# Second MLP's weight sums ordered behind the first MLP's gates, stores ordered behind loads, x loaded in pieces

## The chip, the cores and the metric

The kernel runs on one core of one Trainium2 chip. The metric is the device time of one execution in microseconds; before the change it is 837.95 us, the median of three runs (836.85 to 838.01).

## The reference, cut to what matters

A linear attention feeds two MLPs. q, k and v are float32; the four weight matrices are float64 and reach the chip as their bits:

```
q_s = softmax(q, over head_dim); k_s = softmax(k, over seq)      # 4 batches x 8 heads x 576 x 64
x   = q_s @ (k_s^T v), heads side by side                        # 2304 tokens x 512
h   = x @ w_in;   g = h - tanh(h);            x = g @ w_out      # first MLP, 512 -> 2048 -> 512
h   = x @ w_in2;  g = max(h,0)+log1p(exp(-|h|)); out = g @ w_out2   # second MLP
```

## The kernel before

Every product is made from three float32r matmuls: an operand is split into a high part (a cast on ScalarE) and a low part (a subtraction on VectorE), and high by low, low by high and high by high are summed in PSUM.

**Prologue and first MLP.** The 2304 tokens are cut into five blocks of 512, 256, 512, 512 and 512 (blocks 0 to 4). For each block the loop over 16 slices f of the hidden dimension makes one *step*: `hidden` (L460, 12 matmuls), `gate` (L469 to L472: tanh on ScalarE, g on VectorE, gh on ScalarE, gl on VectorE) and `mid_out` (L487 to L489, 12 matmuls into four PSUM accumulators x). Hidden and gate run two steps ahead of mid_out. Steps are numbered 0 to 79 through all blocks. At a block's last step the four accumulators are evicted to SBUF tiles `x2s` (two buffers; chunks 0 and 2 on VectorE, L496, chunks 1 and 3 on ScalarE, L494), and each is stored to DRAM (`x2d`). The next block's first mid_out waits for these evictions, chunk by chunk. Between the steps, `kv_task` and `x_task` prepare the attention output of the next block.

**Weights of the second MLP.** They are prepared while the first MLP runs, in 16 *pairs* of slices: eight of `w2_in_task` (tiles `rawi`, `sums`) and eight of `w2_out_task` (`rawo`, `sumo`). A pair loads two raw tiles of 0.5 MB, converts float64 bits to float32 (L138 on ScalarE, L143 and L144 on VectorE), makes four sums (they belong to a Strassen-Winograd form of the second MLP's products: seven products instead of eight), splits seven pieces (tiles `stage`, L225 and L226) and stores these to DRAM (`formsi`, `formso`). A task is a generator; the loop calls each running task once per step (`advance`). The table at L702 to L704 starts a pair every three steps from step 28 on. But a scheduler places the instructions of each engine by its own modelled times, and nothing holds a pair's instructions back to the step at which they were written.

**Second MLP.** Three groups s of 768 tokens. `x2_task` loads x from DRAM (tile `xs`, L529) and splits it into seven operands `xf`. Then come units A (hidden products, L557) and units B (output products, L658 to L660): 8 x 7 of each per group. Each unit uses one weight piece `wf` of 256 KB that `load_form` (L549) loads eight units ahead, into a ring of eight buffers. `last_parts` (L639, L640) splits the gates for units B, five units ahead. `last_out` evicts results to tiles `ot` and issues their stores (L677) at once. Group s+1's x is loaded during the units B of group s.

All DMAs are issued by SyncE's queue (SPq), in its order: an issue that waits holds back everything behind it. Engine queues, too, run in the order that the scheduler wrote.

Of the kernel before, what the change touches and what calls it, by code (L numbers as in the profile page):

```python
# [16 lines left out]
ALU = mybir.AluOpType  # L17
# [4 lines left out]
def linear_attention_two_mlps(  # L22
# [28 lines left out]
    nc = tc.nc  # L51
    B, H, S, D = q.shape
    NT, DM = out.shape
# [7 lines left out]
    NC = DM // P  # L61
# [28 lines left out]
    def f32(ap):  # L90
        return ap.bitcast(F32)
# [5 lines left out]
    NFORM = 7  # L97
# [114 lines left out]
    PN = NF // 2  # L212
# [43 lines left out]

    OUT_FORM = (2, 0, 3, 4, 5, 1, 6)

    def w2_out_task(p):

        raws = [raw_tile(f"rawo1_{f}").rearrange("p c f -> p (c f)") for f in PAIRS[p]]
        for raw, f in zip(raws, PAIRS[p]):
            load_out(raw, w2_out, f)
        yield
        yield
        w0, w1 = (convert(raw).rearrange("p (s f) -> p s f", s=2) for raw in raws)
        yield
        sums = f32(raw_tile(f"sumo{p}").rearrange("p c f -> p (c f)")).rearrange("p (s f) -> p s f", s=4)
        t2, t3, t1, t4 = (sums[:, i] for i in range(4))
        b11, b12, b21, b22 = w0[:, 0], w0[:, 1], w1[:, 0], w1[:, 1]  # L270
        nc.vector.tensor_tensor(t1, b12, b11, op=ALU.subtract)
        nc.vector.tensor_tensor(t2, b22, t1, op=ALU.subtract)
        nc.vector.tensor_tensor(t3, b22, b12, op=ALU.subtract)
        nc.vector.tensor_tensor(t4, b21, t2, op=ALU.subtract)
        yield
        split_to(forms[1], p, ((0, w1), (2, w0[:, :1])))
        yield
        split_to(forms[1], p, ((3, sums[:, :2]), (5, sums[:, 2:])))
        yield
# [167 lines left out]

    ghl = {}
    acc = {}
    tanh = [None]  # L450

    def hidden(i, f, step):
        n = SIZES[i]
# [10 lines left out]
    def gate(i, f, h):  # L464
        n = SIZES[i]
        g = main.tile([P, NMAX], F32, tag="g", name=f"g{i}_{f}", bufs=2)[:, :n]
        gh = main.tile([P, NMAX], F32R, tag="gh", name=f"gh{i}_{f}", bufs=3)[:, :n]
        gl = main.tile([P, NMAX], F32R, tag="gl", name=f"gl{i}_{f}", bufs=3)[:, :n]
        tanh[0] = nc.scalar.activation(g, h, AF.Tanh)  # L469
        nc.vector.tensor_tensor(g, h, g, op=ALU.subtract)  # L470
        nc.scalar.copy(gh, g)  # L471
        nc.vector.tensor_tensor(gl, g, f32(gh), op=ALU.subtract)  # L472
        ghl[i, f] = gh, gl

    x2d = [dram.tile([P, NC, n], F32, tag=f"x2d{i}", name=f"x2d{i}") for i, n in enumerate(SIZES)]
# [29 lines left out]
    columns = [[] for _ in range(NS)]  # L505
    chunks = []
    for i in range(NB):
        for j in range(JS[i]):
            s, at_ = divmod(len(chunks), W // P)
# [14 lines left out]
    def x2_task(s):  # L524


        xs = late["xs"].tile([P, NC, W], F32, tag="xs", name=f"xs{s}", bufs=1)
        for i, of, n, to in columns[s]:
            nc.sync.dma_start(out=xs[:, :, to : to + n], in_=x2d[i][:, :, of : of + n])  # L529
        yield  # L530
        b11, b12, b21, b22 = (xs[:, k : k + 2, t : t + HW] for k in (0, 2) for t in (0, HW))
        t1, t2 = (late["xs"].tile([P, 2, HW], F32, tag=f"t{n}", name=f"t{n}_{s}", bufs=1) for n in (1, 2))
        nc.vector.tensor_tensor(t1, b12, b11, op=ALU.subtract)
        nc.gpsimd.tensor_tensor(b12, b22, b12, op=ALU.subtract)
        yield
        nc.vector.tensor_tensor(t2, b22, t1, op=ALU.subtract)
        yield
        for k, of in enumerate((b11, b21, t2, b12, t1, b22)):
            split(s, k, of, nc.vector)
            yield  # L540
            if k == 1:
                nc.gpsimd.tensor_tensor(b21, b21, t2, op=ALU.subtract)
        split(s, 6, b21, nc.vector)

    def load_form(unit):
        kind, n, k = unit[:3]
        t = late["wf"].tile([P, 2, 2 * P], F32R, tag="wf", name="wf_" + "_".join(map(str, unit)), bufs=8)
        of = forms[0][n % PN][:, k] if kind == "A" else forms[1][unit[3]][:, OUT_FORM[k]]
        nc.sync.dma_start(out=f32(t), in_=of)  # L549
        wf[unit] = t  # L550

    def product(a, n, k, first):
        w, x = wf.pop(("A", n, k)).rearrange("p h (c f) -> p h c f", c=2), xf[n // PN, k]
# [87 lines left out]

    NT2 = HW // P
    last = {}

    def last_out(s, k, p):

        if p == 0 and k in (0, 1):
            last["m" if k else "one"] = [
                ps.tile([P, 512], F32, tag=tag, name=f"{'m' if k else 'one'}{s}_{j}", bufs=4 if tag == "acc" else 2)
                for j, tag in enumerate(("acc", "a", "a") if k else ("acc", "acc", "acc"))  # L650
            ]
        g, w = gs.pop((s, k, p)), wf.pop(("B", s, k, p))
        for j in range(NT2):
            one, m = (last[name][j][:, : DM // 2] if name in last else None for name in ("one", "m"))
            a = m if k in (1, 3, 6) else one
            c = slice(j * P, (j + 1) * P)
            first = p == 0 and k in (0, 1, 3)
            nc.tensor.matmul(a, g[:, 1, c], w[:, 0], start=first, stop=False, skip_group_check=True)  # L658
            nc.tensor.matmul(a, g[:, 0, c], w[:, 1], start=False, stop=False, skip_group_check=True)  # L659
            nc.tensor.matmul(a, g[:, 0, c], w[:, 0], start=False, stop=p == PN - 1, skip_group_check=True)  # L660
            if p == PN - 1:
                with tc.high_priority():
                    if k in (0, 2, 4):
                        u = last["u", k, j] = late["g"].tile([P, DM // 2], F32, tag=f"v{k}_{j}", name=f"v{s}_{k}_{j}")
                        nc.scalar.activation(u, one, AF.Copy, scale=1.0 / WS)
                    if k == 5:
                        t = late["g"].tile([P, DM // 2], F32, tag="o", name=f"ot{s}_{k}_{j}", bufs=6)
                        nc.scalar.activation(t, one, AF.Copy, scale=1.0 / WS)
                    elif k in (1, 4, 6):
                        u = last["u", {1: 0, 4: 4, 6: 2}[k], j]  # L670
                        t = late["g"].tile([P, DM // 2], F32, tag="o", name=f"ot{s}_{k}_{j}", bufs=6)
                        nc.vector.scalar_tensor_tensor(t, m, 1.0 / WS, u, op0=ALU.mult, op1=ALU.add)
                if k in (1, 4, 5, 6):
                    half, cols = k in (4, 6), k in (4, 5)
                    i, b = chunks[s * (W // P) + half * NT2 + j]
                    rows = out[BASE[i] + b : BASE[i] + SIZES[i] : JS[i], :]
                    nc.sync.dma_start(out=rows[:, cols * DM // 2 : (cols + 1) * DM // 2], in_=t)  # L677


    running = []  # L680
# [12 lines left out]
    def at(block, step, make):  # L693
        starts.setdefault(block * NF + step, []).append(make)
# [5 lines left out]
        if f >= PRE and f % 2 == 0:  # L700
            at(0, f - 8, lambda f=f: w_task(f // 2))
    for p in range(PN):  # L702
        at(2, 3 * p - 4, lambda p=p: w2_in_task(p))
        at(2, 3 * (PN + p) - 4, lambda p=p: w2_out_task(p))  # L704
    for i in range(NB - 1):
        for hp in range(NHP):
            if i < B - 1:
# [69 lines left out]
    for s in range(NS):  # L777
# [6 lines left out]
        n = (s + 1) * PN  # L784
# [10 lines left out]
    x2 = None  # L795
    loads = iter([u for u in UNITS if u[0] != "M"])
    for n in range(min(starts), NB * NF - 2):
# [14 lines left out]
        while n >= -2 and len(gated) < min(n + 3, len(steps)):  # L812
            i, f = steps[len(gated)]
            gate(i, f, hidden(i, f, len(gated)))
            gated.append((i, f))
        if n >= 0:
            i, f = steps[n]
# [35 lines left out]
    with tc.issue_after(tables.ins):  # L853
        x2 = None
        for unit in UNITS:
            if unit[0] == "M":
                next(first_mlp)
                continue
            if unit == ("A", 0, 5):
                assert next(first_mlp, None) is None  # L860
                main_stack.close()
                stacks["g"] = pool("g")
            if unit[0] == "A":
                _, n, form = unit
                if form == 0:
                    pairs[n] = hidden_pair(n)
                next(pairs[n])
            else:
                _, s, form, p = unit
                if (form, p) == (0, 0):  # L870
                    for ahead in backs[done : done + AHEAD]:
                        last_parts(*ahead[1:])
                    x2 = x2_task(s + 1) if s < NS - 1 else None
                    if x2:
                        next(x2)
                at_ = form * PN + p
                ahead = backs[done + AHEAD] if done + AHEAD < len(backs) else None
                if ahead and ahead[1] == s:
                    last_parts(*ahead[1:])
                done += 1  # L880
                last_out(s, form, p)
                if x2 and at_ in (20, 23, *range(26, 47, 3)):
                    next(x2, None)
            for u in itertools.islice(loads, 1):
                load_form(u)
    for key in ("g", "h", "wf", "xf", "xs"):
        stacks[key].close()

# [31 lines left out]
```

## Time and profile before

| what | us |
|---|---|
| median of three runs | 837.95 |
| profiled execution, its time | 840.5 |
| its span | 838.7 |
| PE (TensorE matmul) busy | 816.2 (97%) |
| DVE (VectorE) busy | 596.7 (71%) |
| ACT (ScalarE) busy | 445.6 (53%) |
| mean granted TensorE clock | 0.996 of full speed |

TensorE is the engine that is nearly always busy, so the profile is read for the places where it waits or runs at its lower clock, and for what stands in the queues of the engines that it waits for. The span leaves out 1.8 us of the execution's own time. Blocks 0 to 4 end at about 133, 192, 292, 391 and 481 us of the span; units A and B follow to the end.

### The profile page before, as it was taken

What the parts mean: (1) busy time and instruction counts of PE and PEld (TensorE: products, weight loads), DVE (VectorE), ACT (ScalarE), POOL (GpSimd) and SP (SyncE); (2) the same over time, 40 slices, a digit from 0 to 9 for tenths busy, and PEclk for the clock granted to TensorE, in tenths of its full rate; (3) what the DMA queues carried; (4) which work ended last, traced back from release to release, by engine and by line L of the source; (5) the groups of instructions that cost most, each with busy time, mean ns of one, the idle gap of its engine ahead of it and who ended that gap; (6) DMA issues with size and microseconds to landing.
All of it is one profiled execution on the core that took longest, in us unless ns stands there. A gap on an engine that the chain in (4) does not pass through costs nothing.

```text
span 838.7 us, 14211 instructions
## 1 busy us (share of the span) xinstructions
PE 816.2 (97%) x5068; PEld 737.1 (88%) x5068; DVE 596.7 (71%) x1134; ACT 445.6 (53%) x791; POOL 28.7 (3%) x46
## 2 busy tenths in 40 slices
PE   7999999999999979999999999999999999999998
PEld 6778888898878768888888899999999999999998
DVE  6899987898789864444253277996278995477963
ACT  4888765765666653232242355755255654355553
POOL 5000000000000000001011000100000000000000
PEclk9999999999999989999999999999999999999999
DMA  9978668778667770003022388787988788888886
GB/s 244 353 222 249 191 213 288 233 236 275 243 237 253 267 267 19 13 14 124 1 76 101 110 260 254 241 264 269 313 254 257 229 272 265 285 253 254 245 262 188
DMA packets 118311, 180.22 MB, mean 215 GB/s; under 512 B 28128, under 2 KB 59360, under 8 KB 118240
## 3 DMA queue, kind: packets, MB, share of 16 engines
q1 hardware_dynamic: 118240, 179.30, 66.8%
q8 instruction: 41, 0.67, 0.3%
q14 instruction: 30, 0.25, 0.1%
HBM read 140.47 MB, written 38.80 MB: 214 GB/s over the span
## 4 chain that ended last, share of the span: by engine, by line
PE 73%; DVE 10%; DMA 8%; ACT 5%; issue 2%; SPq 1%; DVEq 0%; ACTq 0%
PE h L460 16%; PE one L557 10%; PE two L557 8%; PE x L487 5%; PE x L488 5%; PE x L489 5%; PE one L658 3%; PE one L660 3%; PE one L659 3%; DMA rawo<-in_moe_w_out_dram 3%; PE m L658 3%; PE m L660 3%; PE m L659 3%; ACT rawo L138 2%; DVE stage L226 1%
## 5 line engine op out<-in xcount | busy, mean ns | idle before, releaser
L460 PE MATMUL h<-xh,i 128*128 128x512 f32 (+1 forms) x640 | 199.5, 377 | 1.4 <-DVE g L470 1.3
L460 PEld LDWEIGHTS h<-xh,i 128*128 128x128 f32 x640 | 117.9, 190 | 22.9 <-DVE g L470 1.7
L487 PE MATMUL x<-gh,o 128*128 128x512 f32 (+1 forms) x320 | 118.7, 371 | 5.9 <-DVE x2s L496 5.9
L460 PE MATMUL h<-xl,i 128*128 128x512 f32 (+1 forms) x320 | 119.0, 372 | 0.0
L488 PE MATMUL x<-gl,o 128*128 128x512 f32 (+1 forms) x320 | 118.5, 370 | 0.0
L489 PE MATMUL x<-gh,o 128*128 128x512 f32 (+1 forms) x320 | 118.3, 370 | 0.0
L557 PE MATMUL one<-xf,wf_A 128*128 128x384 f32 x576 | 109.0, 335 | 0.2 <-DMA wf_A<-formsi 0.2
L639 ACT CAST gs<-g 128x384 fp32r<-128x384 f32 x144 | 72.6, 512 | 64.9 <-PE one L660 30.1
L557 PEld LDWEIGHTS one<-xf,wf_A 128*128 128x128 f32 x576 | 100.3, 188 | 0.7 <-issue 0.5
L640 DVE TENSOR_TENSOR gs<-g,gs 128x384 fp32r<-128x384 f32 x144 | 79.6, 561 | 27.2 <-ACT gs L639 27.2
L470 DVE TENSOR_TENSOR g<-h,g 128x512 f32<-128x512 f32 (+1 forms) x80 | 50.6, 632 | 63.1 <-ACT g L469 63.1
L469 ACT ACTIVATE g<-h 128x512 f32<-128x512 f32 (+1 forms) x80 | 44.6, 558 | 83.6 <-PE h L460 83.3
L658 PE MATMUL one<-wf_B,gs 128*128 128x256 f32 x288 | 82.0, 285 | 2.2 <-DMA wf_B<-formso 1.4
L557 PE MATMUL two<-xf,wf_A 128*128 128x384 f32 x432 | 83.3, 335 | 0.0
L660 PE MATMUL one<-wf_B,gs 128*128 128x256 f32 x288 | 81.0, 282 | 0.0
L659 PE MATMUL one<-wf_B,gs 128*128 128x256 f32 x288 | 81.0, 282 | 0.0
L487 PEld LDWEIGHTS x<-gh,o 128*128 128x128 f32 x320 | 60.6, 189 | 17.3 <-DVE x2s L496 5.6
L557 PEld LDWEIGHTS two<-xf,wf_A 128*128 128x128 f32 x432 | 75.4, 188 | 0.2
L471 ACT CAST gh<-g 128x512 fp32r<-128x512 f32 (+1 forms) x80 | 46.8, 585 | 47.3 <-DVE g L470 47.0
L489 PEld LDWEIGHTS x<-gh,o 128*128 128x128 f32 x320 | 60.6, 190 | 10.1
L488 PEld LDWEIGHTS x<-gl,o 128*128 128x128 f32 x320 | 60.7, 190 | 9.8 <-DVE gl L472 0.2
L460 PEld LDWEIGHTS h<-xl,i 128*128 128x128 f32 x320 | 60.7, 190 | 9.3
(118 smaller groups left out, 1460.8 us busy)
## 6 DMA issues: line engine op xcount, KB each, us to landing
wf_A<-formsi SPq DMA_DIRECT2D x168, 256.0 KB, 3.2
wf_B<-formso SPq DMA_DIRECT2D x168, 256.0 KB, 3.4
rawo<-in_moe_w_out_dram SPq DMA_DIRECT2D x32, 511.8 KB, 5.9
rawi<-in_moe_w_in_dram SPq DMA_DIRECT2D x32, 511.0 KB, 5.7
formsi<-stage SPq DMA_DIRECT2D x24, 512.0 KB, 3.1
formso<-stage SPq DMA_DIRECT2D x24, 512.0 KB, 3.2
k<-in_k_dram SPq DMA_DIRECT2D x16, 288.0 KB, 4.2
v<-in_v_dram SPq DMA_DIRECT2D x32, 144.0 KB, 3.3
```

The source lines that it names most:

```text
L460: nc.tensor.matmul(p, w[:, c], x[:, c, :n], start=at == 0, stop=at == 3 * NC - 1)
L470: nc.vector.tensor_tensor(g, h, g, op=ALU.subtract)
L471: nc.scalar.copy(gh, g)
L487: nc.tensor.matmul(a, ol[:, s], gh, start=first, stop=False)
L488: nc.tensor.matmul(a, oh[:, s], gl, start=False, stop=False)
L489: nc.tensor.matmul(a, oh[:, s], gh, start=False, stop=last)
L557: nc.tensor.matmul(a, w[:, wp, c], x[:, xp, c], start=first and at == 0, stop=at == 5, skip_group_check=True)
L639: nc.scalar.copy(t[:, 0], of)
L640: nc.vector.tensor_tensor(t[:, 1], of, f32(t[:, 0]), op=ALU.subtract)
L658: nc.tensor.matmul(a, g[:, 1, c], w[:, 0], start=first, stop=False, skip_group_check=True)
L659: nc.tensor.matmul(a, g[:, 0, c], w[:, 1], start=False, stop=False, skip_group_check=True)
L660: nc.tensor.matmul(a, g[:, 0, c], w[:, 0], start=False, stop=p == PN - 1, skip_group_check=True)
```

## The change

Four edits:

1. The tasks of the second MLP's weights are wrapped in `held`: every call of such a task runs under two ordering scopes, so that its ScalarE instructions stand behind the newest tanh and its VectorE instructions behind the newest gl written so far. The table starts each pair one step later (step 29, 32, ... in place of 28, 31, ...).
2. `x2_task` loads x chunk by chunk (four chunks, two token ranges each: eight loads of 128 or 256 KB in place of two of 512 KB and 1 MB); for groups 1 and 2 one chunk per call, at units B 0, 4, 8 and 12, and the later calls come one unit later.
3. Result stores are collected in a list; after each load of a weight piece at most one is issued, ordered behind that load, and only in units A, in the later units of a form, or in the last form.
4. The first five `last_parts` of a group are called in the units A of the group's last pair, in place of all at the group's first unit B.

```
+    def held(task):
+        for at_ in iter(lambda: "held", None):
+            with tc.issue_after(tanh[0].ins), tc.issue_after(gated_last[0].ins):
+                at_ = next(task, "end")
+            if at_ == "end":
+                return
+            yield
...
-        nc.vector.tensor_tensor(gl, g, f32(gh), op=ALU.subtract)
+        gated_last[0] = nc.vector.tensor_tensor(gl, g, f32(gh), op=ALU.subtract)
...
-        for i, of, n, to in columns[s]:
-            nc.sync.dma_start(out=xs[:, :, to : to + n], in_=x2d[i][:, :, of : of + n])
-        yield
+        for c in range(NC):
+            for i, of, n, to in columns[s]:
+                nc.sync.dma_start(out=xs[:, c, to : to + n], in_=x2d[i][:, c, of : of + n])
+            if s:
+                yield
+        if not s:
+            yield
...
+    def store(n):
+        for to, t in stores[:n]:
+            nc.sync.dma_start(out=to, in_=t)
+        del stores[:n]
...
-                    nc.sync.dma_start(out=rows[:, cols * DM // 2 : (cols + 1) * DM // 2], in_=t)
+                    stores.append((rows[:, cols * DM // 2 : (cols + 1) * DM // 2], t))
...
-        at(2, 3 * p - 4, lambda p=p: w2_in_task(p))
-        at(2, 3 * (PN + p) - 4, lambda p=p: w2_out_task(p))
+        at(2, 3 * p - 3, lambda p=p: held(w2_in_task(p)))
+        at(2, 3 * (PN + p) - 3, lambda p=p: held(w2_out_task(p)))
...
+                if n % PN == PN - 1 and form < AHEAD:
+                    last_parts(n // PN, 0, form)
...
-                    for ahead in backs[done : done + AHEAD]:
-                        last_parts(*ahead[1:])
...
-                if x2 and at_ in (20, 23, *range(26, 47, 3)):
+                if x2 and at_ in (4, 8, 12, 21, 24, *range(27, 48, 3)):
...
+            loaded = None
             for u in itertools.islice(loads, 1):
-                load_form(u)
+                loaded = load_form(u)
+            if stores and (unit[0] == "A" or at_ % PN >= 2 or unit[2] == NFORM - 1):
+                with tc.issue_after(loaded.ins) if loaded else ExitStack():
+                    store(1 if loaded else NT2)
```

TensorE's instructions stand in the same order before and after. What moves stands on VectorE, ScalarE and SyncE; three places follow.

VectorE, before, at the end of block 2 (x2s_0 and x2s_2 are the evictions of its chunks 0 and 2, rawo, sumo and stage the weight work, g_1 and gl_1 a gate):

```order
L271 TENSOR_TENSOR sumo_4321<-rawo_0_4191 128x256
L472 TENSOR_TENSOR gl_0_3034<-g_0_3032,gh_0_3033 128x512
L272 TENSOR_TENSOR sumo_4321<-rawo_1_4192,sumo_4321 128x256
L273 TENSOR_TENSOR sumo_4321<-rawo_1_4192,rawo_0_4191 128x256
L274 TENSOR_TENSOR sumo_4321<-rawo_1_4192,sumo_4321 128x256
L226 TENSOR_TENSOR stage_0_4362<-rawo_1_4192,stage_0_4362 128x2x256
L496 TENSOR_SCALAR x2s_0_3086<-x_0_2247 128x512
L470 TENSOR_TENSOR g_1_3076<-h_49_3063,g_1_3076 128x512
L226 TENSOR_TENSOR stage_2_4366<-rawo_0_4191,stage_2_4366 128x256
L143 TENSOR_SCALAR rawo_2_4326<-rawo_2_4326 128x512
L143 TENSOR_SCALAR rawo_3_4327<-rawo_3_4327 128x512
L472 TENSOR_TENSOR gl_1_3078<-g_1_3076,gh_1_3077 128x512
```

After gl_1 come a stage instruction, two conversions (L144) and then x2s_2. The same place with the change:

```order
L245 TENSOR_TENSOR sums_3042<-rawi_15_2914 128x256
L247 TENSOR_TENSOR sums_3042<-rawi_14_2913,rawi_15_2914 128x256
L246 TENSOR_TENSOR sums_3042<-sums_3042,rawi_14_2913 128x256
L248 TENSOR_TENSOR sums_3042<-rawi_14_2913,sums_3042 128x256
L479 TENSOR_TENSOR g_1_3068<-h_49_3055,g_1_3068 128x512
L505 TENSOR_SCALAR x2s_0_3078<-x_0_2239 128x512
L481 TENSOR_TENSOR gl_1_3070<-g_1_3068,gh_1_3069 128x512
L226 TENSOR_TENSOR stage_0_3101<-rawi_14_2913,stage_0_3101 128x2x256
L226 TENSOR_TENSOR stage_6_3105<-rawi_15_2914,stage_6_3105 128x256
L505 TENSOR_SCALAR x2s_2_3090<-x_2_2241 128x512
```

Between the two evictions stood eight other instructions with four conversions of raw weights among them; now three stand there. The weights at this place are the sixth pair's (rawi), where before it was the last (rawo): the whole weight work sits later in the program.

VectorE, before, at the end of block 1:

```order
L470 TENSOR_TENSOR g_0_2107<-h_32_2094,g_0_2107 128x512
L403 TENSOR_TENSOR qn_0_2285<-q_0_2143,qsum_0_2281 128x2x4x64
L247 TENSOR_TENSOR sums_3165<-rawi_0_3013,rawi_1_3014 128x256
L472 TENSOR_TENSOR gl_0_2109<-g_0_2107,gh_0_2108 128x512
L248 TENSOR_TENSOR sums_3165<-rawi_0_3013,sums_3165 128x256
L496 TENSOR_SCALAR x2s_0_2169<-x_0_1441 128x256
```

The same place with the change; this is the first pair's conversion:

```order
L481 TENSOR_TENSOR gl_0_2103<-g_0_2101,gh_0_2102 128x512
L143 TENSOR_SCALAR rawi_4_2046<-rawi_4_2046 128x512
L143 TENSOR_SCALAR rawi_5_2047<-rawi_5_2047 128x512
L144 SCALAR_TENSOR_TENSOR rawi_4_2046<-rawi_4_2046 128x512
L144 SCALAR_TENSOR_TENSOR rawi_5_2047<-rawi_5_2047 128x512
L505 TENSOR_SCALAR x2s_0_2160<-x_0_1441 128x256
```

Here four conversions now stand between the gate and the eviction of chunk 0; one sum stood there before.

SyncE, before, in the units B of group 0, forms 4 to 6 (wf_B and wf_A are weight pieces, xs is the x of group 2, ot the results):

```order
L529 DMA xs_6774<-x2d_86 128x4x512
L549 DMA wf_B_5_2_5829<-formso_76 128x512
L549 DMA wf_B_5_3_5846<-formso_77 128x512
L549 DMA wf_B_5_4_5860<-formso_78 128x512
L549 DMA wf_B_5_5_5874<-formso_79 128x512
L549 DMA wf_B_5_6_5891<-formso_80 128x512
L677 DMA out_dram<-ot_4_0_5901 128x256
L677 DMA out_dram<-ot_4_1_5909 128x256
L677 DMA out_dram<-ot_4_2_5917 128x256
L549 DMA wf_B_5_7_5920<-formso_81 128x512
```

The same stretch with the change:

```order
L539 DMA xs_6786<-x2d_86 128x512
L563 DMA wf_B_5_3_5855<-formso_77 128x512
L563 DMA wf_B_5_4_5872<-formso_78 128x512
L563 DMA wf_B_5_5_5886<-formso_79 128x512
L539 DMA xs_6786<-x2d_85 128x256
L563 DMA wf_B_5_6_5900<-formso_80 128x512
L539 DMA xs_6786<-x2d_86 128x512
L563 DMA wf_B_5_7_5929<-formso_81 128x512
L661 DMA out_dram<-ot_4_0_5910 128x256
L563 DMA wf_B_6_0_5944<-formso_74 128x512
L563 DMA wf_B_6_1_5958<-formso_75 128x512
L563 DMA wf_B_6_2_5975<-formso_76 128x512
```

The one 1 MB load has become pieces with weight loads between them, and the three stores no longer stand in a row ahead of a weight load.

## Rows read from the trace of the kernel before

**Rows 1.** The page: busy time, and the clock in 40 slices of the span.

```profile
PE 816.2 (97%) x5068; PEld 737.1 (88%) x5068; DVE 596.7 (71%) x1134; ACT 445.6 (53%) x791; POOL 28.7 (3%) x46
PEclk9999999999999989999999999999999999999999
```

**Rows 2.** Waits of TensorE, whole span: us in total, times, longest.

```profile
PE x L487 <- DVE x2s L496: 5.9, 3, 3.5
PE one L658 <- DMA wf_B<-formso: 1.4, 1, 1.4
PE m L658 <- DMA wf_B<-formso: 0.7, 1, 0.7
```

**Rows 3.** Busy time by stretch: PE, PEld, DVE, ACT, POOL, clock, DMA share, GB/s.

```profile
160.00:300.00 140.00, 134.11 (x797) 111.21 (x796) 120.68 (x267) 92.67 (x156) 0.83 (x5) 1.00 0.73 254
320.00:470.00 150.00, 150.00 (x670) 124.20 (x669) 61.46 (x87) 46.48 (x75) 7.37 (x3) 1.00 0.14 46
```

**Rows 4.** Waits of all engines from 284 to 312 us, the end of block 2.

```profile
PE x L487 <- DVE x2s L496: 4.4, 2, 3.5
```

**Rows 5.** The chain of waits from 300 to 330 us: start, us, what.

```profile
301.84 0.43 PE x L488
...
303.97 0.85 PE pt L414 x4
304.82 3.82 PE h L460 x12
308.65 0.23 PE x L487
...
312.07 2.76 PE h L460 x12
...
328.43 0.44 PE pt L414 x4
```

**Rows 6.** ACT and DVE at the end of block 2: start, us, instruction, [idle before <-releaser].

```profile
293.83 0.65 ACT L225 CAST stage<-rawo 128x512 fp32r<-128x512 f32 x1 [2.97 <-DMA formso<-stage]
...
299.10 1.29 DVE L144 SCALAR_TENSOR_TENSOR rawo<-rawo 128x512 uint32<-128x512 uint32 x2
300.31 0.68 DVE L496 TENSOR_SCALAR x2s<-x 128x512 f32<-128x512 f32 x1
```

**Rows 7.** PE and ACT at the end of block 0 and inside block 1.

```profile
130.84 1.39 ACT L138 ACTIVATE rawi<-rawi 128x512 f16<-128x512 bf16 x1 [1.11 <-DMA rawi<-in_moe_w_in_dram]
...
134.81 0.39 PE L487 MATMUL x<-gh,o 128*128 128x256 f32 x1 [1.53 <-DVE x2s L496]
...
162.63 1.40 ACT L138 ACTIVATE rawi<-rawi 128x512 f16<-128x512 bf16 x1
...
165.89 0.30 PE L333 MATMUL pm<-ident,m 96*128 96x96 f32 x1 [1.46 <-ACT kv L361]
```

**Rows 8.** Units B of group 0: DVE, SPq, and a stretch as in Rows 3.

```profile
577.74 0.96 DVE L533 TENSOR_TENSOR t<-xs 128x768 f32<-128x768 f32 x1 [2.46 <-DMA wf_B<-formso]
...
586.81 2.19 SPq L677 DMA_DIRECT2D out_dram<-ot  x3
...
590.00:595.00 5.00, 5.00 (x37) 5.00 (x38) 0.41 (x1) 0.48 (x1) 0.00 (x0) 1.00 1.02 334
```

**Rows 9.** Conversions of the second MLP's raw weights on ACT: ns min/median/max, first to last start.

```profile
L138 ACT ACTIVATE rawi<-rawi x16: 1334/1383/1409, 88.4 to 196.7; 128x512 f16<-128x512 bf16 x16
L138 ACT ACTIVATE rawo<-rawo x16: 1347/1375/1397, 209.9 to 298.3; 128x512 f16<-128x512 bf16 x16
```

**Rows 10.** End of block 1 on DVE and PE, and how long x2d stores take to land.

```profile
191.47 0.42 DVE L496 TENSOR_SCALAR x2s<-x 128x256 f32<-128x256 f32 x1 [0.44 <-PE x L489]
...
196.87 0.42 DVE L496 TENSOR_SCALAR x2s<-x 128x256 f32<-128x256 f32 x1 [0.30 <-DMA x2d<-x2s]
...
197.53 0.40 PE L487 MATMUL x<-gh,o 128*128 128x512 f32 x1
...
x2d<-x2s SPq DMA_DIRECT2D x4, 128.0 KB, 3.7
```

More of the change, by code (lines that the diff above doesn't have):

```diff
@@ L449, in linear_attention_two_mlps @@
     acc = {}
-    tanh = [None]
+    tanh, gated_last = [None], [None]
     def hidden(i, f, step):
@@ L548, in load_form @@
         of = forms[0][n % PN][:, k] if kind == "A" else forms[1][unit[3]][:, OUT_FORM[k]]
-        nc.sync.dma_start(out=f32(t), in_=of)
         wf[unit] = t
+        return nc.sync.dma_start(out=f32(t), in_=of)
     def product(a, n, k, first):
@@ L643, in linear_attention_two_mlps @@
     last = {}
+    stores = []
+    def store(n):
+        for to, t in stores[:n]:
+            nc.sync.dma_start(out=to, in_=t)
+        del stores[:n]
     def last_out(s, k, p):
```

## The prediction

> **What bounds the kernel now.** I read the page first. TensorE is busy 97% of the span, and its clock row shows one slice of 40 below full speed [rows 1]. TensorE's own instructions keep their order, so the change can only remove or add pauses of TensorE and stretches at its lower clock. The second view was therefore the list of TensorE's waits. Outside the prologue three entries matter: 5.9 us in three waits on the eviction `x2s` of a block's accumulators, and 1.4 and 0.7 us on weight pieces `wf_B` [rows 2]. The third view, busy time by stretch, says why evictions come late: from 160 to 300 us VectorE is busy 120.7 of 140 us (86%) and ScalarE 92.7 (66%), while from 320 to 470 us TensorE has no pause at all and VectorE works 61.5 of 150 us (41%) [rows 3]. Fourth I read the neighbourhood of each wait.
>
> *End of block 2.* 4.4 of the 5.9 us lie here [rows 4]. ScalarE waited 2.97 us for a store of `formso` before it could split another weight piece, and VectorE's second eviction, at 300.31, comes right behind two weight conversions that took 1.29 us [rows 6]. After the wait the chip runs TensorE at a lower clock for a while: six matmuls of x at 0.43 us instead of 0.23 (1.20 us lost), four `pt` in 0.85 instead of 0.44 (0.41), twelve of `hidden` in 3.82 instead of 2.76 (1.06) [rows 5]. That is 2.7 us on top of 4.4: 7.1 us in all.
>
> *End of block 0 and inside block 1.* At 134.81 TensorE waited 1.53 us for an eviction; just before, ScalarE held a conversion `rawi` of 1.39 us, itself late for a load. At 165.89 TensorE waited 1.46 us for `kv`, with a conversion of 1.40 us begun at 162.63 in ScalarE's queue [rows 7].
>
> *Units B of group 0.* Beside the 2.1 us of [rows 2], VectorE waited 2.46 us for x of the next group, and SyncE needed 2.19 us for a row of three result stores that stood ahead of weight loads [rows 8].
>
> **The change part by part.**
>
> *Edit 1, weight sums behind the gates, pairs from step 29.* It adds and removes no instruction of VectorE, ScalarE or TensorE. Before, the conversions of the pairs ran from 88.4 to 196.7 and from 209.9 to 298.3 us [rows 9]: 88.4 us for seven distances between eight pairs, some 12.6 us a pair, far ahead of the table. With the change a pair can't start before its step. Steps are about 5.5 us apart (block 3, from 292 to 391 us, is 16 steps with some attention work, 6.2 each; block 4, to 481 us, 5.6 each), so a pair takes 16 to 18 us, the first starts near 190 us and the last ends near 475 us. Some nine of the 16 pairs move behind 320 us, where VectorE has room.
>
> Gains. The wait and the low clock at the end of block 2: by the order only three instructions, none a conversion, stay between the evictions there, so I count all 7.1 (bounds 3.5, if half comes back, to 7.1). The waits at 134.81 and 165.89 lie before the first pair can start: 1.53 + 1.46 = 3.0 (bounds 1.5, since the loads or the attention work may delay the same instructions, to 3.0).
>
> Costs. (a) End of block 1: four conversions, at most 2 x 1.29 = 2.6 us [rows 6], now stand ahead of x2s_0, which began at 191.47. Its tile is free again only when its store has landed (3.7 us in the median; here 191.89 to 196.57, 4.7), and x2s_2 waits for that. Chunk 2's first matmul came at 197.53, 0.24 us after x2s_2 ended [rows 10]; so up to 2.6 - 0.2 = 2.4 us can show. The conversions can begin as soon as their raws land and VectorE waited 0.44 us there; I take 0.9 (bounds 0 to 2.4). (b) End of block 3: two splits and a sum now stand around evictions where the stretch showed no wait; at worst the first wait of block 2 with its clock, 3.5 + 2.7 = 6.2, at best 0. I take 0.4, near the row that shows no wait in 320 to 470 us [rows 3]. (c) Gates: a conversion of ScalarE, 1.38 us [rows 9], may now delay a gh by its length; nine pairs have two each. A gate is made two steps, some 11 us, ahead of its use, and its own chain of four instructions, each no longer than the 0.65 to 0.68 us of the 128x512 rows [rows 6], takes about 3 to 4 us with its waits, so 7 us are left and I take 0.4 (bounds 0 to 13; the upper one is a rival below). (d) Seam: the last pair ends in steps 77 to 79, where the splits stand ahead of the last gates and four stores of `formso` ahead of the first weight loads of the second MLP; I take 0.5 (bounds 0 to 7.1, the price of block 2's end).
>
> *Edit 2, x in pieces.* SyncE issues 18 DMAs more, at some 0.5 us each on a queue that is not full. The gain is that a weight piece waits behind 128 or 256 KB and not behind 1 MB. *Edit 3, stores behind loads.* The three-store rows go. Together I take 1.6 of the 2.1 us [rows 2] (bounds 0 to 2.1): some weight load will still come late, since in 590 to 595 us the queues already move 334 GB/s [rows 8]. The same rows show pieces of 256 KB reaching that rate.
>
> The Trainium skill, "DMA: Bandwidth & Descriptors", section Bandwidth, speaks against pieces: "Batch DMAs to ≥1 MiB for ≥75% of peak." The trace does not bear it out in this stretch, where weight pieces of 256 KB move at 334 GB/s; several are in flight at a time. By the rule the pieces would cost bandwidth; what that would come to is worked out among the rivals.
>
> *Edit 4, first parts in the last pair.* The same instructions, written earlier, stand in nearly the same places of VectorE's and ScalarE's order: 0 (bounds -0.5 to +0.5, less than one split).
>
> Sum: gains 7.1 + 3.0 + 1.6 = 11.7; costs 0.9 + 0.4 + 0.4 + 0.5 = 2.2; net 9.5 us. The profiled execution took 840.5 us (span 838.7 and 1.8 around it) and is 2.55 above the median of the runs, 837.95. Against the profile that is 831.0; taken off the median it is 828.5, and this is the forecast.
>
> **Rivals.**
>
> *The boundaries keep half.* x2s has two buffers, so chunk 2 can't be evicted before chunk 0's store has landed, with or without weight work. For it: at the end of block 1 VectorE waited on that very store [rows 10]. Against: there TensorE lost nothing by it. Half of 7.1 + 1.5 stays, 4.3 us: about 832.5.
>
> *Slower: late gates or late attention work in the gap-free stretch.* The weight work enters 320 to 470 us, where TensorE has no pause to lose it in [rows 3]. If each of nine pairs costs TensorE what a conversion cost it at 165.89, 1.46 us [rows 7], that is 13.1 us: 828.5 + 13.1 = 841.6. It decides from 9.5 / 9 = 1.06 us a pair. Against: VectorE is 59% idle there, and gates have some 7 us to spare.
>
> *A stall at the seam* of the two MLPs as large as that of block 2, with its clock: 7.1 instead of 0.5, so 835.1.
>
> *Pieces are slower.* If the x of two groups (3.1 MB) moved at 254 GB/s [rows 3] and not 334 [rows 8], it would take 12.4 in place of 9.4 us, and weight pieces behind it would be late by that 3.0: 831.5.
>
> That is the case that the rule of the Trainium skill, "DMA: Bandwidth & Descriptors", would bring.
>
> *The change doesn't do what it says*: the waits come back at other places with the low clock behind them, and nothing is left: 838.
>
> **How the numbers follow.** Forecast 0.55 (its own range 825 to 831.5: the lower end if no cost shows and the profile's excess of 2.55 is a pause that goes too, the upper if (a) shows fully and edits 2 and 3 bring nothing); boundaries keep half 0.15; seam 0.10; gates 0.10; nothing left 0.07; pieces 0.03. The runs before spread over 1.2 us, so 0.2%, 1.7 us, is about what a measurement of this kernel can tell from no change. Faster by more (under 836.3): 0.55 + 0.15 + 0.10 + 0.03 = 0.83; within it 0.07; slower 0.10. The range reaches from 824.5 to 837.5; it leaves out the slower case and part of "nothing left".
>
> **What would show it.** Right: no entry of `x2s` over 1 us among TensorE's waits at the end of block 2, full clock in that slice; conversions `rawi` from about 190 us on and `rawo` up to about 470; VectorE's busy share under 75% in 160 to 300 us, and near 75% in 320 to 470 us (61.5 us, and nine pairs of some 5 us: in 160 to 300 us it had 120.7 - 0.41 x 140 = 63 us beyond that level, for some 11 pairs and the attention work); no wait on `wf_B` over 0.5 us in group 0. Wrong: new waits of x on gh or gl, or of h on an operand, between 310 and 470 us (gates); an `x2s` wait at the end of block 1 or 3 (terms a and b); a pause of over 2 us between 465 and 495 us (seam); or waits on `wf` that grow while the GB/s of the units B falls (pieces).

## The result

The changed kernel takes 828.53 us in the median of 4 runs (827.87 to 831.16); the kernel before, in the same comparison, 837.98 (4 runs, 836.85 to 842.76). The ratio is 0.9882, with a 95% interval of 0.9838 to 0.9927: 9.5 us less, against a forecast of 828.5.

The page of the kernel after, its busy times and its clock row, to be put beside [rows 1]:

```profile
PE 811.6 (98%) x5068; PEld 735.0 (89%) x5068; DVE 596.3 (72%) x1134; ACT 445.8 (54%) x791; POOL 28.9 (4%) x46
...
PEclk9999999999999999999999999999999999999999
```

VectorE and ScalarE do the same work as before. TensorE's busy time is 4.6 us shorter; its slow slice, 2.7 us by [rows 5], is gone. TensorE's waits over the whole span, as in [rows 2] (us in total, times, longest):

```profile
PE pm L342 <- DVE m L327: 4.7, 1, 4.7
PE one L570 <- ACT u L589: 1.3, 1, 1.3
PE h L469 <- DVE g L479: 1.3, 1, 1.3
PE one L677 <- ACT v L684: 1.1, 1, 1.1
...
PE one L570 <- DVE ot L691: 0.4, 1, 0.4
```

No entry on x2s (5.9 us before), none on kv, none on wf_B. Three entries are new: 1.3 us on `u` at the seam of the two MLPs, and 1.1 us on `v` and 0.4 on `ot` in the units B of group 0. The two stretches of [rows 3], now:

```profile
160.00:300.00 140.00, 140.00 (x809) 117.48 (x809) 100.12 (x215) 78.09 (x134) 0.47 (x4) 1.00 0.51 169
...
320.00:470.00 150.00, 149.90 (x676) 125.08 (x675) 104.08 (x187) 80.26 (x125) 7.41 (x3) 1.00 0.61 220
```

The third figure is VectorE's busy time: 120.7 us fell to 100.1 (72%) in the first stretch and 61.5 rose to 104.1 (69%) in the second; TensorE now works through both. The conversions of raw weights, as in [rows 9], begin 96 us later and end 148 us later:

```profile
L138 ACT ACTIVATE rawi<-rawi x16: 1358/1374/1440, 184.2 to 310.6; 128x512 f16<-128x512 bf16 x16
L138 ACT ACTIVATE rawo<-rawo x16: 1356/1368/1449, 325.9 to 445.8; 128x512 f16<-128x512 bf16 x16
```

Since TensorE's 5068 recorded matmuls stand in one order in both traces, their starts can be subtracted one by one. The second column below is how far TensorE gained in that place (minus: lost), worked out in this way.

| place (time before) | gained, us | forecast |
|---|---|---|
| end of block 0 (135) and inside block 1 (166) | 1.7 + 1.6 | 3.0 |
| attention work in block 2 (249 and 275) | 0.6 + 0.8 | 0 |
| end of block 2 with its slow clock (280 to 320) | 7.7 | 7.1 |
| end of block 1 (190 to 200) | 0 | -0.9 |
| end of block 3 (390) | -0.4 | -0.4 |
| seam (470 to 490) | -1.2 | -0.5 |
| units B of group 0 (560 to 605) | 1.1 | 1.6 |

These two executions differ by 12.6 us in their times (840.5 and 827.92), the medians by 9.5; how much of that is known, the clock section below says.

### The profile page after: what moved, and what is told of

It is laid out like the page before. It is cut to its first block, busy times and chain, and to the rows that moved or that the text cites. A ratio compares the mean times of both kernels' runs of the same rounds, so it can differ in the third digit from the quotient of the medians.

```text
span 826.1 us, 14230 instructions
## 1 busy us (share of the span) xinstructions
PE 811.6 (98%) x5068; PEld 735.0 (89%) x5068; DVE 596.3 (72%) x1134; ACT 445.8 (54%) x791; POOL 28.9 (4%) x46
## 4 chain that ended last, share of the span: by engine, by line
PE 86%; DVE 6%; DMA 4%; ACT 2%; issue 1%; SPq 1%; ACTq 0%; DVEq 0%
PE h L469 21%; PE one L570 10%; PE two L570 8%; PE x L496 7%; PE x L497 7%; PE x L498 7%; PE one L677 4%; PE one L679 3%; PE one L678 3%; PE m L679 3%; PE m L677 3%; PE m L678 3%; PE px L449 2%; PE pk L360 2%; PE idle L772 1%; DMA wf_A<-formsi 1%
## 5 line engine op out<-in xcount | busy, mean ns | idle before, releaser
L481 DVE TENSOR_TENSOR gl<-g,gh 128x512 fp32r<-128x512 f32 (+1 forms) x80 | 52.8, 659 | 41.8 <-ACT gh L480 41.3
```

The lines of the kernel that those rows point to most:

```text
L481: gated_last[0] = nc.vector.tensor_tensor(gl, g, f32(gh), op=ALU.subtract)
```

## What the experiments asked

The execution's first 90 us, the prologue, vary by themselves: the 501st matmul of TensorE starts between 88.6 and 93.5 us, in kernels whose compute instructions stand in the same order up to there. In the longest, that of edit 1 alone, TensorE's granted clock was 0.50 to 0.52 of full speed from 15 to 25 us, the lower of its two levels; in the kernel before it was 1.00 there. The table therefore has, beside median and ratio, the time from the 501st matmul's start to the last matmul's end in the profiled execution ("rest"). By this measure the kernel before has 746.4 and the changed one 733.8. The median of before was 840.17 beside the first four runs, 839.18 beside the next four and 839.56 beside the last four. The ratio is that of the runs of one comparison, with its 95% interval, and not the quotient of the two medians.

| kernel | median | ratio to before | rest |
|---|---|---|---|
| edit 1 alone | 831.41 | 0.9887 [0.9858, 0.9916] | 734.7 |
| without edit 1 | 838.54 | 0.9974 [0.9957, 0.9991] | 743.0 |
| no scopes | 837.24 | 0.9975 [0.9954, 0.9996] | 742.1 |
| scopes, a pair every 2 steps | 838.21 | 0.9968 [0.9948, 0.9987] | 742.0 |
| scopes, pairs 3 steps earlier | 828.75 | 0.9876 [0.9850, 0.9903] | 733.6 |
| x in two loads | 829.52 | 0.9880 [0.9855, 0.9905] | 734.3 |
| stores at once | 829.40 | 0.9893 [0.9858, 0.9929] | 733.7 |
| first parts late | 829.73 | 0.9886 [0.9860, 0.9912] | 735.1 |
| more DMA | 835.24 | 0.9941 [0.9919, 0.9963] | 741.8 |
| x's preparation held | 825.08 | 0.9828 [0.9801, 0.9855] | 730.3 |
| same, pairs 1 step earlier | 824.73 | 0.9822 [0.9803, 0.9840] | 730.0 |
| edit 1 and x's preparation held | 827.49 | 0.9858 [0.9838, 0.9879] | 731.8 |

## Experiments: which edit, and by what

**Edit 1 alone.** The kernel before with `held` and the later table:

```
+        at(2, 3 * p - 3, lambda p=p: held(w2_in_task(p)))
+        at(2, 3 * (PN + p) - 3, lambda p=p: held(w2_out_task(p)))
```

> The kernel before with edit 1 alone (weight sums held behind the gates, pairs one step later). Theory A (edit 1 carries the gain: its weight work no longer stands ahead of x2s and kv): 828 to 830.5 us against 838, no TensorE wait on x2s or kv between 120 and 450 us, full clock there; the waits on wf_B in the units B of group 0 stay, some 2 us. Rival B (the DMA edits 2 and 3 carry half): 833 or more.

831.41 is above the 828 to 830.5 of theory A and below rival B's 833. But the kernel before, too, took 840.17 in this comparison, and the ratio, 0.9887, is that of the changed kernel, 0.9882. The profiled execution, the slowest of the six, had a prologue 4.7 us longer than that of before; its rest, 734.7, is within 0.9 us of the changed kernel. As expected, the waits on x2s and kv are nearly gone (0.2 us of x2s stay) and the one on a weight piece stays:

```profile
PE one L667 <- DMA wf_B<-formso: 2.3, 1, 2.3
...
PE x L496 <- DVE x2s L505: 0.2, 1, 0.2
```

**Without edit 1.** The changed kernel with the old table and tasks not wrapped.

> The changed kernel without edit 1: x in pieces, stores behind loads, first parts in the last pair, and the weight work as before. Theory A: 836 to 838.5 us, with the x2s wait of 4 to 6 us and the slow stretch at the end of block 2, and the waits on wf_B gone. Rival B: 833 or less.

838.54, as theory A has it: edits 2 to 4 alone bring 0.26% (0.09 to 0.43), and x2s is waited for 5.4 us. Edit 1 is the change.

**No scopes.** `held` is taken away, the table's later start stays: `at(2, 3 * p - 3, lambda p=p: w2_in_task(p))`, likewise for the second table line.

> The changed kernel with the pairs one step later in the table, but without the two ordering scopes around their calls. Theory A (the scopes hold the work; the scheduler hoists it otherwise): as without edit 1, 836 to 838.5 us, rawi conversions starting near 90 us. Rival C (the table's later start is what spreads the work): as the changed kernel, 828 to 830 us, rawi from about 185 us.

Rival C falls. Up to 380 us VectorE's and ScalarE's instructions stand in the very order of the kernel before, the conversions run where they ran before, and TensorE waits for x2s as before:

```profile
L138 ACT ACTIVATE rawi<-rawi x16: 1332/1374/1402, 89.5 to 199.2; 128x512 f16<-128x512 bf16 x16
L138 ACT ACTIVATE rawo<-rawo x16: 1341/1382/1407, 211.8 to 299.5; 128x512 f16<-128x512 bf16 x16
```

```profile
PE x L496 <- DVE x2s L505: 6.3, 3, 3.5
```

**A pair every two steps.** Scopes kept: `at(2, 2 * p - 3, ...)` and `at(2, 2 * (PN + p) - 3, ...)`.

> The changed kernel with the same scopes, but a pair every two steps in place of three, so that the weight work is half as dense again and ends near 390 us. Theory A, where the place behind the gates decides: within 1 us of the changed kernel, and the pause at the seam of the MLPs (1.33 us) gone or smaller. Rival D, where the lower density of the weight work decides: VectorE again above 80% busy from 190 to 390 us, x2s or kv waits of 2 us or more back, 831 or more.

Theory A, as I had put it, falls: with every weight instruction still behind its gate, nearly all of the gain is lost. Rival D does not hold in its own words either, since VectorE is not above 80% busy: from 200 to 400 us it works 151.5 us (76%), in the changed kernel 143.8 (72%). What differs more is the waits of weight instructions for their own DMAs. Their rows between 88 and 460 us, first of the kernel before, then of the changed one, then of this one:

```profile
ACT stage L225 <- DMA formso<-stage: 10.6, 6, 3.2
...
ACT rawi L138 <- DMA rawi<-in_moe_w_in_dram: 4.0, 4, 1.6
...
ACT rawo L138 <- DMA rawo<-in_moe_w_out_dram: 2.0, 5, 0.6
```

```profile
ACT stage L225 <- DMA formso<-stage: 1.9, 3, 0.8
```

```profile
ACT stage L225 <- DMA formsi<-stage: 8.7, 8, 2.7
ACT stage L225 <- DMA formso<-stage: 8.4, 9, 1.6
ACT rawo L138 <- DMA rawo<-in_moe_w_out_dram: 7.0, 11, 1.5
ACT rawi L138 <- DMA rawi<-in_moe_w_in_dram: 6.5, 6, 2.5
...
DVE rawo L143 <- DMA rawo<-in_moe_w_out_dram: 1.8, 4, 0.9
```

With the smaller rows these are 19.4, 1.9 and 33.8 us. A pair takes seven tiles of one ring of six buffers (two raw, one of sums, four `stage`), and each is free only after a load has landed and been used or a store has landed. Asked for every two steps, the pairs outrun these DMAs, and their instructions stand waiting at the head of ScalarE's and VectorE's queues; what is behind them waits too. VectorE at the end of block 3 in this kernel:

```profile
387.20 0.69 DVE L226 TENSOR_TENSOR stage<-sumo,stage 128x512 fp32r<-128x512 f32 x1 [0.84 <-ACT stage L225]
388.78 0.43 DVE L143 TENSOR_SCALAR rawo<-rawo 128x512 uint32<-128x512 uint32 x1 [0.89 <-DMA rawo<-in_moe_w_out_dram]
389.12 0.68 DVE L505 TENSOR_SCALAR x2s<-x 128x512 f32<-128x512 f32 x1
```

The eviction at 389.12 stands behind two weight instructions that waited 0.84 and 0.89 us, one for a cast that itself waited for a store, one for a load. TensorE waited 1.04 us for it, 2.84 us for the next one at 393.68, and then fell to its lower clock (0.66 of full speed in the mean from 395 to 400 us). Between these two evictions stand six instructions, none of which waited for a DMA (the largest idle time is 0.35 us, for a conversion on ScalarE): the second wait is what the late first eviction and the queue's own length make. That the waits on DMAs decide is therefore a reading of these rows, and I take it as theory E for the runs that follow. The Trainium skill, "PSUM — Partial Sum Buffer", section Engine vs sequencer instructions, says that these engines' queues are strictly first in, first out; the rows agree.

**Pairs three steps earlier**, spacing and scopes kept: `at(2, 3 * p - 6, ...)`.

> The changed kernel with every pair three steps earlier (26, 29, ...), scopes and spacing kept. Theory E (the wait that reaches TensorE is a weight instruction that waits for its own DMA in ScalarE's or VectorE's queue; three steps a pair give the DMAs time to land): these waits stay under 5 us in sum, no x2s wait over 1 us, and the pause at the seam (1.33 us) goes, since the last stores of formso leave some 16 us earlier: 1 to 1.5 us under the changed kernel. Rival F (the phase of the pairs against the ends of blocks is what counts, and step 29 happens to fit): x2s or kv waits of 1 us or more back, 830 to 835.

The phase does not matter much (rival F falls): the waits on DMAs are 2.4 us in sum, the time is the same, 828.75. 1.2 us are lost between 180 and 200 us, at the end of block 1, where TensorE waits 0.6 for x2s, and 1.5 are won at the seam (below).

**More DMA.** Behind each raw load, SyncE issues a copy that nobody reads:

```
+            with tc.issue_after(loaded.ins):
+                nc.sync.dma_start(out=idle, in_=w2_out[f * P : (f + 1) * P])
```

> The changed kernel with 1 MB more of DMA a pair: behind each raw load SyncE issues a copy of 0.5 MB from DRAM to DRAM that nobody reads; ScalarE's and VectorE's weight work is the same. Theory E (head of the queue waits for a DMA): the waits of weight instructions on their DMAs, 1.9 us in sum in the changed kernel and 19.4 before, rise above 10 us, and waits of TensorE on x2s or kv of 1 us or more come back: 831 or more. Rival H (where the instructions stand among the gates is all that matters, the DMAs don't): within 1 us of 828.5.

The time went up as theory E says (835.24), but not by the way it says: the weight instructions waited only 3.6 us for their DMAs, not over 10. What was late is the eviction itself, for the store of its buffer's last content:

```profile
386.95 0.69 DVE L511 TENSOR_SCALAR x2s<-x 128x512 f32<-128x512 f32 x1 [1.58 <-DMA x2d<-x2s]
```

TensorE waited 2.0 us there. Another 1.3 us went to `pt`, which waited for `qn`: the added issues also moved some of VectorE's instructions of the attention and twelve of TensorE's matmuls, and behind two of its pauses TensorE ran at its lower clock (0.58 from 389 to 393 us, 0.57 from 573 to 577), so this run does not isolate one cause. It shows that an end of a block can pay for a busier DMA through the two buffers of x2s; that it pays through waiting weight work, as theory E has it, this run does not show.

The kernel before has both at the end of block 2. The store of chunk 0 landed there at 299.18 us, 3.4 us after its issue (2.2 in the changed kernel), and the eviction into the same buffer began only at 300.31, behind two conversions [rows 6]. So of the wait of 3.47 us some 1.1 go to the conversions; the rest is the slower store and the late eviction of chunk 0, for which TensorE had already waited 0.94 us. How the gain of edit 1 divides between the order, the waiting weight instructions and the landing of x2d's stores is not settled.

## Experiments: the smaller edits and the waits that came

**X in two loads**, edit 2 undone; **stores at once**, edit 3 undone (`nc.sync.dma_start(...)` in place of `stores.append(...)`); **first parts late**, edit 4 undone.

> The changed kernel without edit 2: x loaded in two transfers again. If the pieces keep weight loads on time, waits on wf_B of 1 to 2 us come back in the units B of group 0 (+0.5 to +1.5 us); if the pieces only delay x itself (the 1.09 us wait on v behind the cast of x), that wait goes and the time falls by 0 to 1 us.

> The changed kernel without edit 3: results stored as soon as they are evicted. If three stores ahead of a weight load cost what the kernel before showed, the wait of 0.66 us on wf_B near 590 us of before comes back and little else: +0.3 to +1.5 us; if the pieces alone cured it: 0.

> The changed kernel without edit 4: the first five splits of a group's gates are called at its first unit B again. If the edit moves nothing that TensorE waits for: within 0.5 us of the changed kernel, the same waits. Rival: the splits come late for the first units B, which then wait 0.5 to 2 us in each of three groups.

None can be told from the changed kernel by its time (829.4 to 829.7, intervals that overlap). In the traces edit 2 trades one wait for another: without it the 1.1 us on `v` go and this comes back:

```profile
PE one L673 <- DMA wf_B<-formso: 1.6, 1, 1.6
```

Nothing of this kind comes back with the stores at once; the parts called late lengthen the waits on `u` and `v` to 2.0 and 1.6 us in that one execution, and the rest by 1.3 us.

**X's preparation held.** The wait on `v`, in ScalarE's queue of the changed kernel: the cast `xf` of group 2's x has been placed into group 0's units B, waits there, and holds back what PSUM needs. The row names a weight piece; the cast reads none, so I take the wait to be for the load of x, which stands in the same DMA queue.

```profile
564.41 0.83 ACT L529 CAST xf<-xs 128x768 fp32r<-128x768 f32 x1 [1.11 <-DMA wf_B<-formso]
565.15 0.51 ACT L652 CAST gs<-g 128x384 fp32r<-128x384 f32 x1
565.56 0.93 ACT L684 ACTIVATE v<-one 128x256 f32<-128x256 f32 x3
```

If so, this is the same fault as that of the weights, and the same scopes should mend it:

```
+                    with tc.issue_after(newest_gs[0].ins), tc.issue_after(newest_gs[1].ins):
                         next(x2, None)
```

> The changed kernel with the preparation of the next group's x (t, xf) held behind the newest gate split gs, by the same kind of scopes. If the waits on v (1.09 us) and ot (0.38) in group 0 come from x's preparation waiting for its DMA in the queues, both go: 1 to 1.5 us under the changed kernel. Rival: the preparation, now bunched at the end of units B, makes the next group's first units wait: 0 to +5 us.

825.08, 3.5 us under the changed kernel's median (from another comparison) where 1 to 1.5 were expected: the waits on v and ot went (1.8 us by the matmuls' starts) and two of 0.5 on `gs` as well, 2.9 us in all. After 100 us a single wait of TensorE is left (the page's threshold for such rows is 0.2 us):

```profile
PE one L571 <- ACT u L590: 1.1, 1, 1.1
```

**The same with edit 1 only**, edits 2 to 4 left out:

> The kernel before with edit 1 and x's preparation held behind the gate splits, without edits 2 to 4. If the wait on wf_B that edits 2 and 3 took away (2.28 us with edit 1 alone) comes from x's preparation and its 1 MB load at that place, holding it cures that wait too: 825 to 827 us. Rival: the 1 MB load and the three stores still delay weight loads: 828 to 830, wf_B waits of 1 us or more.

827.49, between both: a wait on wf_B of 1.3 us stays. Beside edit 1 and the held preparation the DMA edits are worth some 1.5 us of the rest (731.8 against 730.3).

**The seam.** `u` waits in ScalarE's queue behind a cast of a gate that VectorE could not write:

```profile
476.17 0.96 DVE L629 SCALAR_TENSOR_TENSOR g<-hh,e 128x768 f32<-128x768 f32 x1 [3.41 <-DMA wf_A<-formsi]
```

The row names a weight load, which this gate does not read. The gates' memory is that of the first MLP's last tiles, and the last of the four stores x2d there landed at 475.9 us, 0.3 us before the gate began. These stores took 4.7 us to land (2.4 before), with the last pair's stores issued at 457 us and the DMA engines 75% busy from 455 to 470. In the kernel with pairs three steps earlier they are 48% busy there, the stores land in 2.5 us, and there is no pause; VectorE's row names the store:

```profile
473.01 0.96 DVE L629 SCALAR_TENSOR_TENSOR g<-hh,e 128x768 f32<-128x768 f32 x1 [1.21 <-DMA x2d<-x2s]
```

Hence the last kernel: preparation held and pairs from step 28.

> The changed kernel with x's preparation held behind the gate splits (825.1 us as an edit by itself) and all pairs one step earlier (28, 31, ...). If the pause at the seam (1.1 to 1.3 us, g waits for the last stores of x2s) comes from the last pair's formso stores crowding the DMA queues there: 823.5 to 824.5. Rival: the x2s wait at the end of block 1 that came with three steps earlier (0.6 us) comes here too and takes the gain back: 825 to 825.5.

824.73: no pause at the seam, but 0.8 us on x2s at the end of block 3 in its place. Within the spread it is the held preparation's 825.08. Both kernels' slowest runs (825.33 and 825.23) are below the changed kernel's fastest (827.87), and their rests are 3.5 and 3.8 us shorter; the comparisons are different ones, though, and the intervals of the ratios overlap.

## The clock after a pause is not the same each time

In the kernel before, without edit 1 and without scopes, TensorE has the same pause of 3.46 or 3.47 us at the end of block 2; VectorE's and ScalarE's instructions stand in the same order in all three up to there. Busy times and granted clock from 298 to 312 us in the three, in that order (the eighth figure, behind the counts, is the clock):

```profile
298.00:312.00 14.00, 10.96 (x38) 8.89 (x39) 10.42 (x19) 7.57 (x13) 0.00 (x0) 0.76 0.64 251
```

```profile
298.00:312.00 14.00, 10.54 (x42) 8.26 (x41) 11.04 (x21) 8.62 (x16) 0.00 (x0) 0.88 0.71 277
```

```profile
298.00:312.00 14.00, 10.53 (x49) 8.32 (x48) 11.85 (x23) 9.37 (x17) 0.00 (x0) 1.00 0.76 286
```

38, 42 and 49 matmuls fit into these 14 us. Counted from the first matmul behind the pause, TensorE needs 15.21, 14.06 and 12.47 us for the next 56. The 2.7 us of slow clock that I read in [rows 5] are thus what one execution paid; another pays 1.6, another nothing. That last one ran at the lower clock elsewhere, at 0.50 from 137 to 140 us, behind a wait of 2.2 us for x2s. The prologues of the two profiled executions of before and after are within 0.2 us of each other, so their difference of 12.6 us lies wholly behind it, with 2.7 us of slow clock in it. Why the medians differ by only 9.5 the executions without a profile do not show.

## Why the prediction was right

- *Bound.* TensorE, held up at block ends and in group 0: right; all the gain lies in the places named, and in two that were left at zero (1.4 us of the attention work). That the weight work had delayed these two is not shown: the kernel without scopes, with the same order of instructions there as before, has neither pause.
- *Edit 1, gains.* 7.1 and 3.0 forecast; 7.7 and 3.3 in the two traces, but up to 2.7 of the 7.7 is a clock that is not always lost. The mechanism was right only by half: I ascribed the gain to what stands in the queue, [rows 6], and to VectorE's free time. The runs show that the order is needed (no scopes: 0.9975 of before, no more than edits 2 to 4 bring) and does not suffice (every two steps: 0.9968); the pairs must also stand far enough apart. That it is the DMAs' pace that sets this distance fits the rows (1.9 us of waits on DMAs against 33.8), but the run that was to isolate it did not. The row was there: ScalarE's 2.97 us for a store of `formso`.
- *Cost (a), end of block 1, 0.9.* Did not come (0): the four conversions had their raws in time. The eviction behind them came 1.5 us later against TensorE's matmuls than before, but its store landed in 1.9 us, not in the 4.7 that the term had taken over from before. It came, as 1.2 us, with pairs three steps earlier.
- *Cost (b), 0.4.* Came as 0.4. *(c), gates, 0.4.* Did not come: from 320 to 470 us TensorE has no wait on a gate, so the slower rival falls.
- *Cost (d), seam, 0.5.* Mis-sized: 1.2. The stores of `formso` were named, and they act through the landing of x2d.
- *Edits 2 and 3, 1.6.* 1.1 in the trace, because new waits on `v` (1.1) and `ot` (0.4) took back part of what the waits on wf_B gave; by time neither edit shows alone (edits 2 to 4 together, without edit 1, bring 0.26%). The rival by the rule of the Trainium skill, "DMA: Bandwidth & Descriptors", section Bandwidth, did not come: with x in two large loads the time was 829.52, no less than with pieces.
- *The boundaries keep half.* No: no entry on x2s is left. The buffer that this rival names is close to setting the time, though: at the end of block 2 chunk 0's store now lands at 288.48 us, and chunk 2's eviction begins at 288.58. (Its sum, 828.5 + 4.3, is 832.8, not 832.5.)
- That the sum came out at the forecast to 0.03 us is chance: the medians of before moved by 2 us between comparisons.

## What to carry to other kernels

Background work put into the queues of engines that also serve the critical path must not wait there: look for its own waits on DMAs, not only for its busy time, and pace it by its buffers. Here the pace was shown to matter; that it matters by these waits is the best reading of the rows, not a proof. An ordering scope pins such work, and the same scope mended a second place that the change itself had opened. Where the start of a program varies, compare kernels from a fixed instruction on.

## What was unexpected of the hardware

The stores of 256 KB at the seam landed in 2.4 to 2.5 us in three kernels (before, and the two with pairs three steps and one step earlier) and in 4.7 us in the changed one, with the DMA engines 78% to 84% busy meanwhile in all four, so this share by itself does not tell the two apart. The same pause of 3.5 us, with the same instructions in the same order around it, left a mean granted clock of 0.76, 0.88 or 1.00 over 14 us. The prologue's length varied by 4.9 us between executions, in the longest with 10 us at the lower clock.
